# Attention kernel: batch 0's products of probabilities and values, split into three parts

## The chip, the cores and the metric

The kernel runs on one core of a Trainium2 chip. The core has five engines that work side by side, each through its own instructions in a fixed order: TensorE (PE, the matmuls; PEld is its weight loads), VectorE (DVE), ScalarE (ACT), GpSimd (POOL) and SyncE (SP, which here only issues transfers). The metric is the device time of one execution in microseconds. Before the change the median of three runs is 521.31 us (519.27, 521.31 and 526.38). The profiled execution took 525.91 us, of which 524.1 us lie between its first and its last instruction.

## The reference

Four batches, eight heads each, 576 positions, 64 numbers per head, all in float32:

```python
scores = q @ k.T / sqrt(64)
scores = where(causal, -1e9, scores + min(-(cum_i - cum_j), 0))   # cum: running sum of max(s, 0)
attn   = softmax(scores)
x      = attn @ v                       # the heads side by side: 4 x 576 x 512
gate   = sigmoid(conv5(x))              # over the five last positions, per channel
x      = (gate * (x @ w_val)) @ w_out
h      = relu(x @ w_in);  u, v = the two halves of h
out    = (u * (w_spatial @ layernorm(v) + b)) @ w_out2
```

The weights arrive as 64-bit floats. The kernel turns them into float32 on the chip and multiplies `moe_w_out` by `moe2_w_in` once (the "fold"), one half of it in plain float32 (`wo_f`, `wi_f`, line 429), the other half as sums of two reduced-precision numbers.

## The kernel before, in words

The attention runs in **turns**, `w` = 0 to 32, one head each (lines 693 to 733). Turn `w` issues the scores of head `w` and the transposes of head `w - 1`.

*Scores* (lines 190 to 225). A head's 576 queries are cut into five tiles, of 64, 128, 128, 128 and 128 queries. For each, TensorE fills a PSUM bank (`pss`), VectorE adds the mask and finds the row's extreme (line 219, `p` and `nm`), and ScalarE takes the exponential and the row's sum (line 224). The first eight heads, batch 0, multiply in float32 (line 209); the others in two steps (lines 211, 212). The tiles `p` exist twice, for even heads (buffers p_116 to p_120) and odd ones (p_127 to p_131).

*Transposes* (lines 257 to 272). TensorE turns `p` block by block into `pst`, and ScalarE copies it to `pt` (line 272), in four banks: bank 1 and 2 hold the keys 0 to 127 (`c` = 0), bank 3 those of `c` = 2 and 3, bank 0 those of `c` = 1 and 4. There are two `pt`, so the copies for head `h + 2` wait until head `h`'s has been read. A new `p` of head `h + 2` waits for the transposes that read that of head `h`.

*Products with the values* (`pv`, lines 276 to 300) are made for two heads at a time. For every `c` and each head `j` one matmul, with the 64 columns of `vraw` as weights, adds to `pso` (queries 128 to 575: 448, 448, 320, 192 and 64 columns) or makes `psq` (queries 0 to 127); head 0 writes the PSUM partitions 0 to 63 and head 1 the others. Line 294 holds all of them back until the first of them, of `c` = 1 and head 1, can go. VectorE then scales by the inverse sums `R` into `x` (line 300). `R` is transposed to `psr`, copied by ScalarE, written to DRAM (`r_d`, line 242) and read back on SP (line 248). `pso` exists once and `psq` shares one bank with `psr`.

*Behind it.* The convolution reads `x` (lines 309 to 313). The rest (the fold, the gate's product, the mixing) is issued between the pieces of attention by `more`, whose share per turn is a table: 3 in batch 0, then 11.5, 10, 7.6 and 6. During batch 0 it is the preparation of the weights (lines 357 to 409: loads `wg` and `wr` on SP, steps on ScalarE, VectorE and GpSimd), the float32 half of the fold (`fold`, evacuated as `wch` by ScalarE and `wcl` by VectorE) and the first products with `w_val` (`xvh`, `xvl`, lines 417 to 419).

*The order of the work.* The program is written as above, and a scheduler (line 787) then sets the order of each engine's instructions by its own model of their times and by the program's priorities. Each engine runs its list strictly in order, so an instruction that waits holds all behind it.

Of the kernel before, what the change touches and what calls it, by code (L numbers as in the profile page):

```python
# [7 lines left out]
F32 = mybir.dt.float32  # L8
# [4 lines left out]
ALU = mybir.AluOpType  # L13
PSUM = bass.MemoryType.PSUM

NEG = -1.0e30
NATIVE = 8


F64_LOW = 2.0 ** (896 // 8 - 127 + 16)  # L20
# [4 lines left out]
def tile_stickbreak_attention_moe(  # L25
# [18 lines left out]
    NH, S = s.shape  # L44
    B = out.shape[0]
    H = NH // B
# [11 lines left out]
    BLK, w = {}, 0  # L58
# [5 lines left out]
    V, G, A, T, SY = nc.vector, nc.gpsimd, nc.scalar, nc.tensor, nc.sync  # L64
# [162 lines left out]
    R = {}  # L227
# [48 lines left out]
    def pv(h):  # L276

        b, p = h // H, (h % H) // 2
        x = X[b, p] = early.tile([128, S], F32, tag=f"x{p}", name=f"x{p}", bufs=1)
        r = R.pop(h // 2).rearrange("p i q -> p (i q)")  # L280
        pts = [PT.pop(h + j) for j in range(2)]
        vs = [vraw.pop(h + j) for j in range(2)]

        first = None
        for tag, q0, q1 in (("o", 128, S), ("q", 0, 128)):
            po = ps.tile([128, 512], F32, tag=tag, name=f"ps{tag}", bufs=1)
            cs = [1, 0, 2, 3, 4] if q0 else [0]
            for c in cs:
                a = max(q0, c * 128)
                o = BLK[c, c] + a - c * 128  # L290
                for j in (1, 0):
                    with ExitStack() as es:
                        if first is not None:
                            es.enter_context(tc.issue_after(first))
                        m = T.matmul(po[64 * j:64 * j + 64, a - q0:q1 - q0], vs[j][:, c, :], pts[j][:, o:o + q1 - a],  # L295
                                     start=c == cs[0], stop=c == cs[-1])
                    first = first or m.ins
            for a, e in ((q0, 64), (64, q1)) if q0 == 0 else ((q0, q1),):
                o = a + 64 if a else 0
                V.tensor_tensor(out=x[:, a:e], in0=po[:, a - q0:e - q0], in1=r[:, o:o + e - a], op=ALU.mult)  # L300

    Z = {}

# [312 lines left out]
    def more(n):  # L616
        with tc.high_priority(offset=0):
            more_(n)
# [74 lines left out]
    for w in range(NH + 1):  # L693
        if w == H + 1:
            queue.clear()
            queue.append(start())
        elif w % H == 1 and w > 1 and w < NH:
            queue += [mixing_a(w // H - 1), mixing_b(w // H - 1)]
        if w >= NATIVE:
            load(w + 2)  # L700
        n_g = [3, 11.5, 10.0, 7.6, 6.0][0 if w <= H else 1 if w <= H + 4 else 2 if w <= 2 * H else 3 if w <= 3 * H else 4]
        gs = [n_g / 5] * 5
        if w < NH:
            scores(w, [0, 1])
        if w > 0:
            transposes(w - 1, [1, 2])
        if w % 2 == 0 and w > 0:
            lay_sums(w // 2 - 1)
        more(gs[0])
        if w < NH:  # L710
            scores(w, [2])
        prep(w + 1)
        if w > 0:
            transposes(w - 1, [3])
        more(gs[1])
        if w < NH:
            scores(w, [3])
        if w > 0:
            transposes(w - 1, [0])
        if w % 2 == 0 and w > 0:  # L720
            spread_sums(w // 2 - 1)
        more(gs[2])
        if w < NH:
            scores(w, [4])
            if w < NATIVE:
                load(w + 2)
            if w % 2:
                normalise(w // 2)
        more(gs[3])
        if w % 2 == 0 and w > 0:  # L730
            pv(w - 2)
            conv((w - 2) // H, ((w - 2) % H) // 2)
        more(gs[4])
    load_ahead(wo_d, B - 2, ["wv", "wv"])
# [56 lines left out]
```

## Time and profile before

| what | value |
|---|---|
| median of three runs | 521.31 us (519.27 to 526.38) |
| profiled execution | 525.91 us, span 524.1 us |
| PE busy | 495.5 us, 95% |
| PEld busy | 412.9 us, 79% |
| ACT busy | 334.3 us, 64% |
| DVE busy | 312.9 us, 60% |
| POOL busy | 125.1 us, 24% |
| mean granted TensorE clock | 0.977 |

The first row says how much a difference must be to be seen: the three runs lie 7 us apart. Busy shares are means over a program of two halves, with batch 0 (about the first 109 us) unlike the rest, so they are read by stretches. The granted clock is a share of 2.4 GHz; 0.50 is 1.2 GHz.

### The profile page before, as it was taken

How to read it: one execution, taken by the hardware profiler on the slowest of the kernel's cores; microseconds unless marked ns; L12 is line 12 of the kernel's file. 1: busy time of each engine (PE TensorE's matmuls, PEld its weight loads, DVE VectorE, ACT ScalarE, POOL GpSimd, SP SyncE). 2: the span in 40 equal slices, each digit the busy share in tenths (PEclk: the TensorE clock that was granted, in tenths of full speed). 3: DMA queues.
4: the chain of work that ended last, by engine and by line, in shares of the span. 5: the costliest groups of instructions: out<-in, count | busy, mean ns of one | idle time of the engine just before them, and what ended most of it. 6: DMA issues, size and time to landing. Idle time of an engine off the chain costs nothing.

```text
span 524.1 us, 9075 instructions
## 1 busy us (share of the span) xinstructions
PE 495.5 (95%) x3186; PEld 412.9 (79%) x3186; DVE 312.9 (60%) x830; ACT 334.3 (64%) x813; POOL 125.1 (24%) x167
## 2 busy tenths in 40 slices
PE   7789787969999999999999999999999999999997
PEld 5445445558877978989979897899579889998997
DVE  6777877676888878564477644835289544025120
ACT  3997785596685976985648754876279834224322
POOL 5211111014172111300335021002115013046140
PEclk9989997989999999999999999999999999999999
DMA  7837774345546374067631322286220060700002
GB/s 210 272 103 252 232 233 153 107 139 155 151 159 215 89 236 153 3 201 237 202 103 58 107 83 84 60 279 216 77 67 14 26 255 24 240 0 3 1 1 91
DMA packets 28302, 69.26 MB, mean 132 GB/s; under 512 B 4000, under 2 KB 12352, under 8 KB 28256
## 3 DMA queue, kind: packets, MB, share of 16 engines
q1 hardware_dynamic: 23328, 63.88, 39.0%
q10 hardware_dynamic: 4928, 4.80, 2.7%
q8 instruction: 25, 0.41, 0.3%
q14 instruction: 21, 0.17, 0.1%
HBM read 55.96 MB, written 9.16 MB: 124 GB/s over the span
## 4 chain that ended last, share of the span: by engine, by line
PE 64%; DVE 13%; ACT 10%; DMA 8%; issue 3%; POOL 1%; SPq 1%; DVEq 0%; ACTq 0%; POOLq 0%
PE psm L417 11%; PE psm L419 11%; PE psm L418 11%; PE pso L295 7%; PE pst L271 6%; PE psm L593 3%; PE psm L595 3%; PE psm L594 3%; DVE p L219 3%; DVE z L312 2%; ACT p L224 2%; PE pss L211 2%; PE pss L212 2%; DMA R<-r_d 2%; DMA wr<-in_w_out 2%
## 5 line engine op out<-in xcount | busy, mean ns | idle before, releaser
L224 ACT ACTIVATE p<-p,nm 64x64 f32<-64x64 f32 (+4 forms) x160 | 88.4, 553 | 10.0 <-DVE nm L219 9.7
L271 PE MATMUL pst<-ident,p 128*128 128x128 f32 x480 | 81.4, 281 | 9.4 <-ACT p L224 6.0
L272 ACT ACTIVATE pt<-pst 128x512 f32<-128x512 f32 (+1 forms) x128 | 61.0, 497 | 42.7 <-PE psq L295 25.7
L219 DVE CUSTOM_DVE_ANT_0 p<-pss,mask 64x64 f32<-64x64 f32 (+4 forms) x160 | 64.0, 419 | 25.4 <-PE pss L212 15.7
L271 PEld LDWEIGHTS pst<-ident,p 128*128 128x128 f32 x480 | 59.0, 143 | 23.2 <-ACT p L224 10.2
L312 DVE SCALAR_TENSOR_TENSOR z<-x,cw,z 128x575 f32<-128x575 f32 (+3 forms) x64 | 54.3, 854 | 4.7 <-ACT z L309 4.2
L79 POOL TENSOR_TENSOR y<-gt,y 128x288 fp32r<-128x288 f32 x32 | 27.8, 872 | 115.7 <-ACT y L72 115.7
L79 POOL TENSOR_TENSOR g<-gt,g 128x288 fp32r<-128x288 f32 x32 | 27.1, 849 | 104.1 <-ACT g L72 104.0
L295 PE MATMUL pso<-pt,vraw 128*64 128x448 f32 (+3 forms) x320 | 51.8, 431 | 0.0
L211 PE MATMUL pss<-qk 128*64 128x64 f32 (+1 forms) x144 | 46.8, 343 | 1.6 <-DVE nm L219 1.4
L295 PEld LDWEIGHTS pso<-pt,vraw 128*64 128x64 f32 x320 | 23.1, 140 | 25.1 <-issue 17.4
L212 PE MATMUL pss<-kd,cn 66*64 66x64 f32 (+1 forms) x144 | 42.2, 298 | 0.0
L209 PE MATMUL pss<-raw 128*128 128x288 f32 (+4 forms) x96 | 31.2, 425 | 8.0 <-DVE nm L219 7.2
L417 PE MATMUL psm<-g,wch 128*128 128x288 f32 x128 | 38.2, 306 | 0.2 <-ACT u L581 0.2
L593 PE MATMUL psm<-wsh,vh 128*128 128x288 f32 x128 | 38.1, 304 | 0.2 <-ACT u L581 0.2
L595 PE MATMUL psm<-wsl,vh 128*128 128x288 f32 x128 | 37.6, 300 | 0.0
L418 PE MATMUL psm<-g,wcl 128*128 128x288 f32 x128 | 37.4, 298 | 0.0
L594 PE MATMUL psm<-wsh,vl 128*128 128x288 f32 x128 | 37.3, 298 | 0.0
L419 PE MATMUL psm<-g,wch 128*128 128x288 f32 x128 | 37.1, 298 | 0.0
L300 DVE TENSOR_TENSOR x<-pso,R 128x448 f32<-128x448 f32 x16 | 9.9, 622 | 44.5 <-DMA R<-r_d 19.9
L498 DVE TENSOR_TENSOR gt<-psm,z 128x288 f32<-128x288 f32 x32 | 14.2, 452 | 32.7 <-PE psm L419 29.7
L417 PE MATMUL psm<-xvh,wv 128*128 128x288 f32 x96 | 30.6, 322 | 2.7 <-DVE wcl L79 2.7
(168 smaller groups left out, 1324.9 us busy)
## 6 DMA issues: line engine op xcount, KB each, us to landing
raw<-in_qk SPq DMA_DIRECT2D x24, 576.0 KB
wv<-wv_d SPq DMA_DIRECT2D x12, 512.0 KB
wv<-wo_d SPq DMA_DIRECT2D x12, 512.0 KB
vraw<-in_vp SPq DMA_DIRECT2D x32, 160.0 KB
R<-r_d SPq DMA_DIRECT2D x32, 160.0 KB
out<-ot ACTq DMA_DIRECT2D x32, 144.0 KB
cn<-qk SPq DMA_DIRECT2D x24, 144.0 KB
wr<-in_w_in SPq DMA_DIRECT2D x5, 512.0 KB
```

The lines of the kernel that those rows point to most:

```text
L79: eng.tensor_tensor(out=out_, in0=in_, in1=f(hi), op=ALU.subtract)
L211: T.matmul(pst[0:m, o:o + b - a], qa[:, q0:q0 + m], kb[:, a:b], start=True, stop=False)
L219: LAST["V"] = V.tensor_tensor_reduce(out=p[i][0:m, a:b], in0=src, in1=mask[0:m, o:o + b - a], scale=-0.125, scalar=3.0e38 if a == 0 else n ...
L224: A.activation(p[i][0:m, 0:e], p[i][0:m, 0:e], AF.Exp, bias=nm[0:m, i:i + 1], scale=-1.0, accum_out=sm[h // 2 % 2][0:m, h % 2, i:i + 1])
L271: T.transpose(pt[:, o - o0:o - o0 + 128], p[i][:, c * 128:(c + 1) * 128], ident[:, r:r + 128])
L272: A.activation(PT[h][:, o0:end], pt[:, 0:end - o0], AF.Copy)
L295: m = T.matmul(po[64 * j:64 * j + 64, a - q0:q1 - q0], vs[j][:, c, :], pts[j][:, o:o + q1 - a], start=c == cs[0], stop=c == cs[-1])
L312: V.scalar_tensor_tensor(out=z[:, d:], in0=x[:, :S - d], scalar=cw[:, p, k:k + 1], in1=z[:, d:], op0=ALU.mult, op1=ALU.add)
L417: T.matmul(pt, ah, bh, start=j == 0, stop=False)
L418: T.matmul(pt, al, bh, start=False, stop=False)
L419: T.matmul(pt, ah, bl, start=False, stop=j == n - 1)
L593: T.matmul(o, vh[c][:, cs], wsh[:, c, hs[hf]], start=c == 0, stop=False)
```

## The change

Batch 0's four pairs of heads no longer call `pv`. In their turns (`w` = 2, 4, 6, 8) the matmuls of the pair are issued in three parts: those of `c` = 0 (with `psq`) behind the transposes of bank 1 and 2, those of `c` = 2 and 3 behind bank 3, those of `c` = 1 and 4 behind bank 0. The scaling stays where `pv` stood. Within a part head 0 now comes before head 1, the sum begins with `c` = 0 instead of 1, and nothing holds a matmul back until another has gone. The two banks are taken when the first part is issued. From batch 1 on `pv` is as before.

```diff
+PARTS = 8
...
+    PO = {}
+
+    def pv_part(h, cs):
+
+        if h < 0:
+            return
+        if h not in PO:
+            PO[h] = [ps.tile([128, 512], F32, tag=t, name=f"ps{t}", bufs=1) for t in "oq"]
+        po, pq = PO[h]
+        for c in cs:
+            for t, q0, q1 in ((po, 128, S), (pq, 0, 128))[0:2 if c == 0 else 1]:
+                a = max(q0, c * 128)
+                o = BLK[c, c] + a - c * 128
+                for j in range(2):
+                    T.matmul(t[64 * j:64 * j + 64, a - q0:q1 - q0], vraw[h + j][:, c, :], PT[h + j][:, o:o + q1 - a],
+                             start=c == 0, stop=c == 4 or q0 == 0)
+
+    def pv_scale(h):
...
+        for t, q0, a, e in ((po, 128, 128, S), (pq, 0, 0, 64), (pq, 0, 64, 128)):
+            o = a + 64 if a else 0
+            V.tensor_tensor(out=x[:, a:e], in0=t[:, a - q0:e - q0], in1=r[:, o:o + e - a], op=ALU.mult)
...
             transposes(w - 1, [1, 2])
+        parts = w - 2 if w <= PARTS and w % 2 == 0 else -1
         if w % 2 == 0 and w > 0:
             lay_sums(w // 2 - 1)
+        pv_part(parts, [0])
         more(gs[0])
...
             transposes(w - 1, [3])
+        pv_part(parts, [2, 3])
         more(gs[1])
...
             transposes(w - 1, [0])
+        pv_part(parts, [1, 4])
...
         if w % 2 == 0 and w > 0:
-            pv(w - 2)
+            pv(w - 2) if parts < 0 else pv_scale(parts)
             conv((w - 2) // H, ((w - 2) % H) // 2)
```

The instructions of each engine are the same before and after, in number and shape; their order differs on every engine from the first pair on, on TensorE up to about the middle of its list. Lines up to 299 move by 1, later ones by 33; the new matmuls are on line 317, the new scaling on line 333.

**TensorE, the first pair.** Before, its ten matmuls into `pso` stand in one block, the two heads in turn (`pt_299` and `vraw_167` are head 1, `pt_235` and `vraw_163` head 0), between the transposes of head 2:

```order
L271 MATMUL pst_415<-ident_91,p04_120 128x128
L295 MATMUL pso_370<-pt_299,vraw_167 64x448
L295 MATMUL pso_370<-pt_235,vraw_163 64x448
L295 MATMUL pso_370<-pt_299,vraw_167 64x448
L295 MATMUL pso_370<-pt_235,vraw_163 64x448
L295 MATMUL pso_370<-pt_299,vraw_167 64x320
L295 MATMUL pso_370<-pt_235,vraw_163 64x320
L295 MATMUL pso_370<-pt_299,vraw_167 64x192
L295 MATMUL pso_370<-pt_235,vraw_163 64x192
L295 MATMUL pso_370<-pt_299,vraw_167 64x64
L295 MATMUL pso_370<-pt_235,vraw_163 64x64
L271 MATMUL pst_436<-ident_91,p04_120 128x128
```

Now head 0's matmul of `c` = 0 goes alone, a turn earlier, between the transposes of head 1:

```order
L272 MATMUL pst_303<-ident_91,p11_128 128x128
L272 MATMUL pst_303<-ident_91,p12_129 128x128
L317 MATMUL pso_314<-pt_235,vraw_163 64x448
L272 MATMUL pst_333<-ident_91,p12_129 128x128
L210 MATMUL pss_344<-raw0_66 128x448
```

and six of the other nine stand in two groups among head 2's transposes, one head a step ahead of the other; the last three (448 of head 1, 64 of both) follow as a third group five transposes later:

```order
L317 MATMUL pso_314<-pt_299,vraw_167 64x448
L317 MATMUL pso_314<-pt_235,vraw_163 64x320
L272 MATMUL pst_405<-ident_91,p01_117 128x128
L272 MATMUL pst_405<-ident_91,p02_118 128x128
L272 MATMUL pst_405<-ident_91,p03_119 128x128
L272 MATMUL pst_405<-ident_91,p04_120 128x128
L210 MATMUL pss_497<-raw0_66 128x320
L317 MATMUL pso_314<-pt_299,vraw_167 64x320
L317 MATMUL pso_314<-pt_235,vraw_163 64x192
L317 MATMUL pso_314<-pt_299,vraw_167 64x192
L317 MATMUL pso_314<-pt_235,vraw_163 64x448
```

What moved: one matmul to the turn before, and the rest from one block into three groups in the same neighbourhood. The other three pairs have the same groups.

**VectorE, around the scaling of the third pair** (`x_698` before, `x_712` now). Before:

```order
L376 SCALAR_TENSOR_TENSOR wg<-wg 128x512
L300 TENSOR_TENSOR x_698<-pso,R 128x448
L300 TENSOR_TENSOR x_698<-psq,R 128x64 x2
L79 TENSOR_TENSOR qk<-raw_66,qk 64x576
L219 ISA p_131,nm<-pss,mask 128x288
L219 ISA nm 128x1
L376 SCALAR_TENSOR_TENSOR wr<-wa,wr 128x512
L79 TENSOR_TENSOR kd_108<-raw_66,qk 64x576
```

Now:

```order
L409 SCALAR_TENSOR_TENSOR wg<-wg 128x512
L80 TENSOR_TENSOR qk<-raw_66,qk 64x576
L409 SCALAR_TENSOR_TENSOR wr<-wa,wr 128x512
L220 ISA p_130,nm<-pss,mask 128x448
L220 ISA nm 128x1
L80 TENSOR_TENSOR kd_108<-raw_66,qk 64x576
L333 TENSOR_TENSOR x_712<-pso,R 128x448
L333 TENSOR_TENSOR x_712<-psq,R 128x64 x2
L220 ISA p_131,nm<-pss,mask 128x288
L220 ISA nm 128x1
```

What moved: the scaling stands three instructions later, behind `qk`, `wr` and `kd_108`. The first `wcl` after it (the evacuation of the fold's first column) was the twelfth large instruction behind the scaling and is now the sixth, with `qk` and `kd_109` of the next head behind it instead of ahead.

**ScalarE, in the same place.** Before, the step `wr<-wr`, which reads a weight transfer, stands behind both `wch`:

```order
L309 ACTIVATE z<-x_698,cw 128x576
L72 ACTIVATE xvh_928<-x_698 128x576
L72 ACTIVATE qk<-raw_67 128x576 x2
L224 ACTIVATE p_131,sm_113<-p_131,nm 128x576
L252 ACTIVATE wch<-psm 128x512 x2
L379 ACTIVATE wr<-wr 128x512
```

Now it stands between them, ahead of an exponential and of the next head's `qk`:

```order
L342 ACTIVATE z<-x_712,cw 128x576
L73 ACTIVATE xvh_928<-x_712 128x576
L253 ACTIVATE wch<-psm 128x512
L412 ACTIVATE wr<-wr 128x512
L225 ACTIVATE p_131,sm_113<-p_131,nm 128x576
L73 ACTIVATE qk<-raw_67 128x576 x2
L253 ACTIVATE wch<-psm 128x512
```

What moved: a step that waits for a transfer went ahead of four that don't need it. The issue of that transfer on SP moved too, from behind the loads `raw_67` and `cn_107` to ahead of them.

## Rows read from the trace of the kernel before

**Rows 1.** Stretches: length, busy of PE, PEld, DVE, ACT, POOL (count), clock, DMA, GB/s.

```profile
26.00:117.00 91.00, 75.92 (x381) 47.43 (x382) 68.10 (x193) 70.07 (x175) 12.81 (x11) 0.90 0.57 175
117.00:260.00 143.00, 140.28 (x977) 123.57 (x977) 100.21 (x268) 106.27 (x265) 37.53 (x42) 0.99 0.51 161
```

**Rows 2.** PE's waits from 20 to 117 us: total, times, longest.

```profile
PE pss L209 <- DVE nm L219: 7.2, 12, 1.8
PE pst L271 <- ACT p L224: 3.1, 1, 3.1
```

**Rows 3.** Timeline of PE, first pair: start, length, line, matmul, records merged [idle before].

```profile
37.57 4.50 PE L295 MATMUL pso<-pt,vraw 128*64 128x448 f32 x20
```

**Rows 4.** The same view, second pair.

```profile
50.72 2.70 PE L295 MATMUL pso<-pt,vraw 128*64 128x448 f32 x20
```

**Rows 5.** The same view, fifth pair, where single matmuls stand among others.

```profile
131.59 0.29 PE L419 MATMUL psm<-xvl,wv 128*128 128x288 f32 x1
131.82 0.54 PE L295 MATMUL pso<-pt,vraw 128*64 128x192 f32 x2
132.29 0.40 PE L418 MATMUL psm<-xvh,wv 128*128 128x288 f32 x1
132.62 0.33 PE L295 MATMUL pso<-pt,vraw 128*64 128x64 f32 x2
132.88 0.40 PE L419 MATMUL psm<-xvl,wv 128*128 128x288 f32 x1
133.20 0.27 PE L295 MATMUL pso<-pt,vraw 128*64 128x64 f32 x1
133.21 0.32 PE L295 MATMUL psq<-pt,vraw 128*64 128x128 f32 x1
```

**Rows 6.** Stretches, columns as in Rows 1: three at the low clock, two at the high.

```profile
34.00:41.00 7.00, 6.59 (x23) 3.21 (x23) 1.91 (x6) 5.66 (x18) 0.09 (x1) 0.53 0.50 156
46.00:56.00 10.00, 9.43 (x58) 5.46 (x56) 9.66 (x27) 8.85 (x23) 2.69 (x3) 1.00 1.01 300
86.00:92.40 6.40, 5.87 (x18) 4.50 (x19) 2.70 (x10) 3.83 (x11) 0.00 (x0) 0.50 0.33 103
92.40:109.00 16.60, 16.60 (x98) 11.18 (x96) 12.19 (x34) 11.20 (x27) 0.00 (x0) 1.00 0.35 98
113.50:119.20 5.70, 4.28 (x19) 4.28 (x20) 1.79 (x8) 5.69 (x17) 0.47 (x1) 0.50 0.49 184
```

**Rows 7.** Timeline of ACT [idle before <- what ended it].

```profile
42.83 1.20 ACT L272 ACTIVATE pt<-pst 128x64 f32<-128x64 f32 x3 [3.17 <-PE psq L295]
86.60 0.70 ACT L379 ACTIVATE wr<-wr 128x512 int32<-128x512 uint32 x1 [3.52 <-DMA wr<-in_w_in]
```

**Rows 8.** Timeline of DVE, scalings and what stands near them.

```profile
42.47 0.36 DVE L219 CUSTOM_DVE_ANT_0 p<-pss,mask 128x192 f32<-128x192 f32 x1 [6.00 <-PE pst L271]
...
61.48 0.62 DVE L300 TENSOR_TENSOR x<-pso,R 128x448 f32<-128x448 f32 x1 [1.85 <-DMA R<-r_d]
...
76.66 0.62 DVE L300 TENSOR_TENSOR x<-pso,R 128x448 f32<-128x448 f32 x1 [2.58 <-DMA R<-r_d]
...
78.36 0.46 DVE L219 CUSTOM_DVE_ANT_0 p<-pss,mask 128x288 f32<-128x288 f32 x1
...
83.60 0.82 DVE L312 SCALAR_TENSOR_TENSOR z<-x,cw,z 128x574 f32<-128x574 f32 x1
...
85.81 0.67 DVE L79 TENSOR_TENSOR wcl<-psm,wch 128x512 fp32r<-128x512 f32 x1
```

**Rows 9.** Timeline of PE, around the waits near 62 and 86 us.

```profile
62.82 0.75 PE L209 MATMUL pss<-raw 128*128 128x288 f32 x2 [1.59 <-DVE nm L219]
...
86.53 0.61 PE L417 MATMUL psm<-xvh,wv 128*128 128x288 f32 x1 [2.71 <-DVE wcl L79]
...
90.14 4.74 PE L429 MATMUL psm<-wi_f,wo_f 128*128 128x512 f32 x8
```

**Rows 10.** Timeline of SP, the weight transfer that ACT reads at 86.60.

```profile
81.53 0.38 SPq L371 DMA_DIRECT2D wr<-in_w_in  x1
```

More of the change, by code (lines that the diff above doesn't have):

```diff
@@ L300, in pv @@
                 V.tensor_tensor(out=x[:, a:e], in0=po[:, a - q0:e - q0], in1=r[:, o:o + e - a], op=ALU.mult)
+    PO = {}
[13 more added lines that the diff above has]
+    def pv_scale(h):
+        if h < 0:
+            return
+        b, p = h // H, (h % H) // 2
+        po, pq = PO.pop(h)
+        for j in range(2):
+            PT.pop(h + j)
+            vraw.pop(h + j)
+        x = X[b, p] = early.tile([128, S], F32, tag=f"x{p}", name=f"x{p}", bufs=1)
+        r = R.pop(h // 2).rearrange("p i q -> p (i q)")
+        for t, q0, a, e in ((po, 128, 128, S), (pq, 0, 0, 64), (pq, 0, 64, 128)):
+            o = a + 64 if a else 0
+            V.tensor_tensor(out=x[:, a:e], in0=t[:, a - q0:e - q0], in1=r[:, o:o + e - a], op=ALU.mult)
     Z = {}
```

## The prediction, made before the change was run

> **What bounds the kernel now.** I read the table by stretches first [rows 1]: it splits the program into a part that TensorE fills and a part that it doesn't. From 117 to 260 us TensorE is busy for 140.28 of 143 us at clock 0.99, so what happens there hardly moves the end unless TensorE gets more to do. From 26 to 117 us, where batch 0 and the change lie, it is busy for 75.92 of 91 us, and the granted clock is 0.90. So 15.1 us of idle time and about 9 us of lost clock (a tenth of 91) are all that the change could win there, some 24 us, or 4.6% of the run.
>
> Then the waits of TensorE [rows 2]: its pauses from 20 to 117 us are many short ones for VectorE's scan of the scores (7.2 us in 12), and one of 3.1 us for an exponential that stands behind the gate's sigmoid. Third, the timelines around the first block [rows 3, 7, 8]: while TensorE works off the ten products of pair 0 in 4.50 us, ScalarE stands for 3.17 us and VectorE for 6.00 us, both until transposes and `psq` behind the block are through. That is the cost the change can reach. Fourth, the granted clock [rows 6]: three stretches near 0.50 (1.2 GHz), at 34 to 41, 86 to 92.4 and 113.5 to 119.2 us. Each follows a time in which TensorE paused; the second follows the 2.71 us until `wcl` [rows 9]. Last, VectorE's scalings [rows 8]: those of pairs 1 and 2 wait 1.85 and 2.58 us for `R` to come back from DRAM, not for the products.
>
> **The change, part by part.** No instruction is added or removed; all of it is order.
>
> *Products that lose their partner.* In the block head 1 and head 0 alternate, and pair 1's takes 2.70 us at the full clock [rows 4]. It streams 448 + 448 + 320 + 192 + 64 = 1472 columns per head. One product of 192 columns alone keeps TensorE from 131.82 to 132.29, 0.47 us [rows 5]; 2944 columns at that rate would be over 7 us, so in the block the two heads run beside each other, at 2.70 / 1472 = 1.83 ns a column. In the new order head 0's first product is alone (448), head 1's 448 stands with head 0's 320 (448), then 320, 192, 192 and 448 follow with the heads shifted by one (768), then 448 with 64 and 64 (512). I take it that products of different heads still overlap when they are not of one `c`: a `pso` and a `psq` product of different length start 0.01 us apart [rows 5]. The sum is 2176 columns instead of 1472: 704 x 1.83 ns = **1.3 us** more per pair.
>
> *More changes of shape.* Before, a pair had two groups (`pso`, `psq`), now five. What a group costs beyond its columns is read where single products stand among others [rows 5]: 0.47 - 192 x 1.83 ns = 0.12 us, and 0.26 (132.62 to 132.88) - 64 x 1.83 ns = 0.14 us. Three more groups, in and out, are 6 x 0.13 = **0.8 us** per pair. The Trainium skill, in TensorEngine Tiling (Array Packing), under Tiling Modes, Key Properties, says that changing the tiling mode drains TensorE, which speaks against cutting a block up; the rows agree that there is a price. With about 175 ns for a drain, the Trainium skill's figure in TensorE: Matmul & The Clock Gate, under Single matmul latency, the 24 changes would make 4.2 instead of 3.1 us, an estimate that would add 1 us to the sum below at most.
>
> Together 2.1 us per pair, 8.4 us for four. How much of it is on the path:
>
> - The first product (0.82 us and two changes, 1.1 us) goes ahead. Pair 0's falls into the pauses for the scan [rows 2], pair 3's into the 2.71 us before `wcl` [rows 9]. That leaves 1.0 us per pair in the old place.
> - Pair 0: there the clock is 0.53 [rows 6] and the block took 4.50 instead of 2.70 us, so 1.0 becomes 1.6 us. ScalarE and VectorE both wait for what is behind it [rows 7, 8], and that is not released earlier: `psq` and the transposes of `p_117` are still behind all of the products. **+1.6**, bounds 0 and +3.5.
> - Pair 1: VectorE is busy for 9.66 of 10 us from 46 to 56 us [rows 6] and sets the pace. **0**, at most +2.1.
> - Pair 2: its first product waits for pair 1's scaling, which ends at 62.1 us [rows 8]; TensorE is idle from 61.2 to 62.82 anyway [rows 9]. The product and the transposes behind it push the scores by about 0.8 us. The 2.58 us wait for `R` behind it [rows 8] hides this: **0**, at most +1.8.
> - Pair 3: TensorE is busy for all of 92.4 to 109 us [rows 6]. **+1.0**, bounds 0 and +2.1.
>
> *VectorE around pair 2's scaling.* The scaling now has `qk`, `wr` and `kd_108` ahead of it, which fill the wait for `R` (three steps of 0.67 to 0.82 us, like those in rows 8, into 2.58 us); it still goes at 76.66 us. Behind it six instead of twelve steps stand ahead of `wcl`: five of 0.46 to 0.82 us from 77.6 us, so `wcl` starts at about 81 instead of 85.81 us [rows 8], before TensorE comes for its bank at 83.8 us. The 2.71 us pause at that place goes [rows 9]. What is late next: ScalarE now reads the transfer `wr` between the two `wch`. It takes 86.60 - 81.53 = 5.07 us from issue to use [rows 7, 10]; with `wr` and `kd_108` done earlier on VectorE, SP can issue it at about 77 us, and it lands at 82. ScalarE stands for some 3 us, in place of the 3.52 it stood [rows 7], with an exponential, `qk` and the second `wch` queued behind. The second bank then comes free at about 87 us, and the fold's third column, at 90.14 us before [rows 9], can follow at about 87.4. **-2.7**; at worst 0, if the wait for `wr` is the longer one; at best -2.7 and the clock too: 5.87 us of work at 0.50 [rows 6] would take half, another -2.9.
>
> *The sigmoid* moves some exponentials later in ScalarE's list. The pause of 3.1 us [rows 2] and the low clock behind it (4.28 us of work, 2.1 lost [rows 6]) can end better or worse by as much. **0**, bounds -5.2 and +3.
>
> Sum: +1.6 + 1.0 - 2.7 = -0.1 us on 525.9 us, the profiled execution's time (1.8 us outside its span), which lies 4.6 us above the median. On the median that is **521 us: no change that could be told**, since 2% of it, 10.4 us, is about what a measurement of this kernel can tell from none. This case's own range, with one or two of the bounds above at their ends, is 515 to 526.
>
> **The rivals.**
>
> 1. *Slower: the first product holds TensorE.* `pso` exists once, so head 0's early product must wait for the scaling of the pair before, which waits for `R`; TensorE then stands in front of transposes that it used to make in that time. For: two scalings wait for `R` [rows 8]. Against: at both, TensorE or VectorE idles as it is. Price: pair 2 waits from about 60.6 to 62.1 us, 1.5 us. It decides once the wait is as long as the 2.71 us after which the clock was at 0.50 for 6.4 us [rows 6, 9], that is with `R` 1.2 us later; then each hold costs about 2.7 + 2.9 us. One such hold, the products' 2.6 and no gain at `wcl` make +8.2; two make +13.8. Time 529 to 535, say 531.
>
> 2. *Faster: TensorE keeps its clock.* If the shorter pauses leave the clock up, 34 to 41 us gives 3.1 us (6.59 us of work, 0.47 of it lost), 86 to 92.4 us 2.9, 113.5 to 119.2 us 2.1 [rows 6], and the pause before `wcl` 2.7: -10.8, and +2.6 for the products, so 513. Against: the first of them begins before the groups that moved, and only one lone product stands in front of it.
>
> 3. *Nothing happens.* `pso` and `psq` are still finished last, ScalarE's copies for the next head still wait for `psq` [rows 7], and a scheduler has put the groups where the block was. Then the array time is hidden or small, with the reshuffled work behind it as the only difference: 521 to 523.
>
> **How the numbers follow.** The forecast has 0.55, rival 1 0.15, rival 2 0.18, rival 3 0.12. The likeliest time is 521. Rivals 2 and 3 and the low end of the sigmoid's bound reach 512, rival 1 with one hold 530; beyond these lie two holds or all three clocks at once with the sigmoid's pause, less than 2 in 10. Range 512 to 530. Faster by over 2% (below 510.9) needs rival 2 and more: 0.08. Slower by over 2% (above 531.7) is rival 1 with more than one hold: 0.09. Within 2%: 0.83.
>
> **What would show it.** Right: the ten products of a pair take about 3.6 to 4.8 us in all at the full clock; VectorE's wait in front of `p_117` is still near 6 us; no wait in front of pair 2's scaling; TensorE's pause before the first `xvh` product is gone, and ScalarE waits about 3 us for `wr` ahead of the second `wch`. Wrong: a TensorE wait of over 2 us for a scaling in front of a product with 448 columns (rival 1); a clock of 1.00 from 34 to 41 us (rival 2); or a difference that arises after 120 us, where only the scheduler's order of the same work could make it.

## The result, and the profile after

The changed kernel takes **525.67 us** (median of 20 runs, 523.35 to 530.29) against 521.88 us for the kernel before in the same comparison (519.27 to 526.38): a ratio of 1.0072, 95% interval 1.0046 to 1.0098. It is slower by 0.7%, which is within 2% and told apart from no change. The profiled execution of before was one with much time at the low clock, so a second one of the same kernel (`base`, below) stands beside it here: 518.71 us, span 516.9. Runs over 1.5% above the fastest of their kernel (three of before, one of `mid_b`) are left out of all medians and means below.

The head of the page of the changed kernel:

```profile
span 524.0 us, 9074 instructions
## 1 busy us (share of the span) xinstructions
PE 500.2 (95%) x3186; PEld 409.6 (78%) x3186; DVE 316.6 (60%) x830; ACT 334.0 (64%) x813; POOL 127.2 (24%) x167
```

Stretches of the changed kernel, columns as in [rows 1], the last one a spell at the low clock:

```profile
34.00:41.00 7.00, 7.00 (x35) 3.48 (x34) 1.77 (x7) 6.00 (x19) 0.00 (x0) 0.76 0.28 88
86.00:92.40 6.40, 6.40 (x32) 3.29 (x30) 1.75 (x6) 3.79 (x11) 0.00 (x0) 1.00 0.38 135
113.50:119.20 5.70, 5.70 (x48) 5.11 (x44) 4.82 (x15) 5.69 (x13) 1.91 (x2) 1.00 0.28 65
26.00:117.00 91.00, 83.53 (x429) 49.38 (x428) 71.38 (x202) 74.05 (x184) 13.10 (x12) 0.96 0.53 175
117.00:260.00 143.00, 139.22 (x946) 121.97 (x946) 102.00 (x262) 104.26 (x260) 40.91 (x44) 0.99 0.54 167
215.00:225.00 10.00, 8.44 (x50) 7.47 (x49) 5.86 (x21) 9.97 (x25) 0.80 (x1) 0.83 0.47 121
```

The same two long stretches of `base`:

```profile
26.00:117.00 91.00, 78.11 (x436) 52.21 (x437) 74.43 (x208) 76.37 (x193) 16.71 (x16) 0.96 0.59 187
117.00:260.00 143.00, 141.17 (x972) 121.33 (x970) 99.35 (x261) 102.15 (x252) 36.42 (x42) 1.00 0.53 164
```

Until 117 us the changed kernel keeps TensorE busy for 5.4 us more than `base`, at the same mean clock, with nearly as many matmuls done (429 records against 436): more time for the work, fewer pauses. From 117 to 260 us it gets 26 matmul records less done in the same time. That is where it falls behind. Followed matmul by matmul, each counted at its mean cost over the two traces, the changed kernel is 1.0 us behind `base` at 117 us, 0.5 at 190 and 7.8 at 260; from 307 us of `base` on, TensorE's order is the same in both. For what `base` does from 190 to 260 us it takes 7.3 us more: 4.1 of work (1.9 in the products of pairs 7 to 9, seven pieces more, and 1.4 in the matmuls next to pieces), 1.6 of pauses and 1.6 of low clock.

TensorE's waits of the changed kernel from 20 to 117 us (line, engine waited for, us, times, longest), the answer to [rows 2]:

```profile
PE pss L210 <- DVE nm L220: 2.7, 5, 1.1
PE pss L212 <- DVE nm L220: 2.0, 2, 1.4
...
PE pso L317 <- PE pst L272: 0.7, 1, 0.7
```

Its products of pair 0 in the old place (three rows), all of pair 1 (five) and the early one of pair 2, in the timeline of TensorE, the answers to [rows 3, 4]. Two records (x2) are one product:

```profile
33.96 1.40 PE L317 MATMUL pso<-pt,vraw 128*64 128x448 f32 x4
...
37.40 1.46 PE L317 MATMUL pso<-pt,vraw 128*64 128x320 f32 x8
...
39.48 1.08 PE L317 MATMUL pso<-pt,vraw 128*64 128x448 f32 x6
...
45.28 0.97 PE L317 MATMUL pso<-pt,vraw 128*64 128x448 f32 x2
...
48.41 0.97 PE L317 MATMUL pso<-pt,vraw 128*64 128x448 f32 x4
...
50.54 1.30 PE L317 MATMUL pso<-pt,vraw 128*64 128x320 f32 x8
...
53.06 1.08 PE L317 MATMUL pso<-pt,vraw 128*64 128x448 f32 x6
...
54.77 0.44 PE L317 MATMUL psq<-pt,vraw 128*64 128x128 f32 x4
...
59.94 0.94 PE L317 MATMUL pso<-pt,vraw 128*64 128x448 f32 x2 [0.67 <-PE pst L272]
```

Its first product with `xvh` and the fold's third column, the answer to [rows 9]:

```profile
82.66 0.29 PE L450 MATMUL psm<-xvh,wv 128*128 128x288 f32 x1
...
85.18 3.70 PE L462 MATMUL psm<-wi_f,wo_f 128*128 128x512 f32 x8 [0.63 <-DVE wcl L80]
```

The same place in `base`, where the wait for `wcl` stands in front of the first `xvh` product:

```profile
81.19 0.40 PE L417 MATMUL psm<-xvh,wv 128*128 128x288 f32 x1 [1.82 <-DVE wcl L79]
...
83.21 3.60 PE L429 MATMUL psm<-wi_f,wo_f 128*128 128x512 f32 x8
```

ScalarE and VectorE of the changed kernel at the places of [rows 7, 8]:

```profile
41.44 1.20 ACT L273 ACTIVATE pt<-pst 128x64 f32<-128x64 f32 x3 [1.44 <-PE psq L317]
...
80.46 0.68 ACT L412 ACTIVATE wr<-wr 128x512 int32<-128x512 uint32 x1 [2.50 <-DMA wr<-in_w_in]
```

```profile
40.97 0.36 DVE L220 CUSTOM_DVE_ANT_0 p<-pss,mask 128x192 f32<-128x192 f32 x1 [4.16 <-PE pst L272]
...
75.23 0.61 DVE L333 TENSOR_TENSOR x<-pso,R 128x448 f32<-128x448 f32 x1
...
79.51 0.68 DVE L80 TENSOR_TENSOR wcl<-psm,wch 128x512 fp32r<-128x512 f32 x1
```

ScalarE and VectorE behind the first block in `base`, where the clock is 1.00 from 34 to 41 us:

```profile
39.97 1.20 ACT L272 ACTIVATE pt<-pst 128x64 f32<-128x64 f32 x3 [0.97 <-PE psq L295]
```

```profile
39.61 0.36 DVE L219 CUSTOM_DVE_ANT_0 p<-pss,mask 128x192 f32<-128x192 f32 x1 [3.70 <-PE pst L271]
```

Up to here most goes the way of the forecast. What the forecast has no row for comes later. Pair 9 (the tenth) in the changed kernel, TensorE; `psm` rows between the products are left out, the last row is the one behind them:

```profile
259.71 0.97 PE L296 MATMUL pso<-pt,vraw 128*64 128x448 f32 x4
...
261.27 1.83 PE L296 MATMUL pso<-pt,vraw 128*64 128x448 f32 x10
...
264.16 0.54 PE L296 MATMUL pso<-pt,vraw 128*64 128x192 f32 x2
...
265.06 0.33 PE L296 MATMUL pso<-pt,vraw 128*64 128x64 f32 x2
...
265.75 0.33 PE L296 MATMUL pso<-pt,vraw 128*64 128x64 f32 x2
...
266.68 0.43 PE L296 MATMUL psq<-pt,vraw 128*64 128x128 f32 x2
...
267.47 0.43 PE L296 MATMUL psq<-pt,vraw 128*64 128x128 f32 x2
...
267.83 0.50 PE L450 MATMUL psm<-wch,g 128*128 128x512 f32 x1
```

The scheduler has cut these twelve products into seven **pieces** (runs of products with no other matmul between them) among the gated block's matmuls; in the kernel before it were three. In the whole trace the changed kernel has 60 pieces, 19 in batch 0 and 41 behind it; the kernel before has 42, that is 7 and 35. From pair 13 on the order is the same in both. Its first product starts at 370.75 us in the changed kernel (of a span of 524.0, so 153.25 before the end) and at 363.30 us in `base` (of 516.9, 153.6 before the end): all of the loss is made ahead of it.

In between, the changed kernel's TensorE waits for an exponential; the stretch around it is the last one (215 to 225 us, clock 0.83) of the changed kernel's above:

```profile
218.86 0.47 PE L272 MATMUL pst<-ident,p 128*128 128x128 f32 x1 [1.21 <-ACT p L225]
```

Measured in the two traces from each matmul's start to the next one's, with the idle time before the next one counted as a pause and the low clock at half speed taken out, TensorE's work grew by 10.4 us (484.8 to 495.2), its pauses fell by 4.3 (23.4 to 19.1), and the low clock took 1.0 more (4.0 to 5.0): +7.05 us, the difference of the spans. Of the work, batch 0's products have 5.6 us (11.85 to 17.4), the later products 1.3 (41.55 to 42.85), and the other matmuls 3.5, most of it in those that stand next to pieces.

### The profile page after: what moved, and what is told of

Read it like the earlier page. It is cut to its first block, busy times and chain, and to the rows that moved or that the text cites. A ratio compares the mean times of both kernels' runs of the same rounds, so it can differ in the third digit from the quotient of the medians.

```text
span 524.0 us, 9074 instructions
## 1 busy us (share of the span) xinstructions
PE 500.2 (95%) x3186; PEld 409.6 (78%) x3186; DVE 316.6 (60%) x830; ACT 334.0 (64%) x813; POOL 127.2 (24%) x167
## 5 line engine op out<-in xcount | busy, mean ns | idle before, releaser
L345 DVE SCALAR_TENSOR_TENSOR z<-x,cw,z 128x575 f32<-128x575 f32 (+3 forms) x64 | 56.6, 891 | 4.6 <-ACT z L342 4.2
L80 POOL TENSOR_TENSOR g<-gt,g 128x288 fp32r<-128x288 f32 x32 | 28.7, 902 | 118.6 <-ACT g L73 118.2
L296 PE MATMUL pso<-pt,vraw 128*64 128x448 f32 (+3 forms) x240 | 41.3, 436 | 0.0
L531 DVE TENSOR_TENSOR gt<-psm,u 128x288 f32<-128x288 f32 x32 | 14.5, 455 | 32.2 <-PE psm L630 23.3
L450 PE MATMUL psm<-y,wv 128*128 128x288 f32 x96 | 29.8, 311 | 3.9 <-ACT ot L641 3.6
L296 PEld LDWEIGHTS pso<-pt,vraw 128*64 128x64 f32 x240 | 17.5, 140 | 19.7 <-issue 13.7
```

Source lines behind the costliest of these rows:

```text
L80: eng.tensor_tensor(out=out_, in0=in_, in1=f(hi), op=ALU.subtract)
L345: V.scalar_tensor_tensor(out=z[:, d:], in0=x[:, :S - d], scalar=cw[:, p, k:k + 1], in1=z[:, d:], op0=ALU.mult, op1=ALU.add)
L450: T.matmul(pt, ah, bh, start=j == 0, stop=False)
```

## The experiments

Theory A: the end shows the products of batch 0, which take 5.6 us more (5.1 in an expectation below). Theory B: that cost is covered by shorter pauses, and the end shows the order behind batch 0.

Every run comes with its mean granted clock. At half speed below full, (1 - clock) x span is the time lost to the low clock; the mean time less this is called *at full clock* here (for the changed kernel 525.97 - 4.75 = 521.2). In the four comparisons that list its clock the kernel before had 513.6 to 514.3, so tenths are noise, and a kernel's runs scatter by 0.6 to 2.6 us (standard deviation). By the runs the figure takes off too much: from run to run of one kernel, 1 us more of that loss goes with only 0.55 us more of time (95% interval 0.45 to 0.65, from 234 runs in 20 groups); why is not shown. So where two kernels differ in clock, what their orders differ by lies between the difference of the times and that at full clock.

| kernel | pieces, batch 0 + later | median us | ratio (95%) | clock | at full clock |
|---|---|---|---|---|---|
| before | 7 + 35 | 521.6 to 522.6 | 1 | 0.985 | 513.6 to 514.3 |
| the change | 19 + 41 | 525.67 | 1.0072 (1.0046 to 1.0098) | 0.991 | 521.2 |
| serial | 7 + 37 | 525.34 | 1.0064 (1.0033 to 1.0094) | 0.985 | 517.6 |
| pair | 14 + 45 | 532.05 | 1.0195 (1.0151 to 1.0239) | 0.988 | 525.2 |
| parts2 | 9 + 36 | 523.91 | 1.0040 (1.0011 to 1.0069) | 0.983 | 514.7 |
| parts6 | 16 + 55 | 530.35 | 1.0164 (1.0119 to 1.0210) | 0.991 | 526.1 |
| c0first | 7 + 35 | 521.34 | 0.9993 (0.9962 to 1.0023) | 0.985 | 513.7 |
| whole_b | 7 + 12 | 515.88 | 0.9875 (0.9838 to 0.9913) | 0.981 | 505.8 |
| whole_a | 19 + 13 | 508.52 | 0.9742 (0.9704 to 0.9781) | 0.996 | 506.5 |
| mid_b | 7 + 31 | 523.75 | 1.0064 (1.0027 to 1.0101) | 0.981 | 515.1 |
| mid_a | 19 + 33 | 520.99 | 0.9998 (0.9965 to 1.0032) | 0.992 | 517.3 |
| tail_b | 7 + 18 | 511.02 | 0.9806 (0.9757 to 0.9855) | 0.986 | 504.0 |
| tail_a | 19 + 24 | 517.20 | 0.9909 (0.9873 to 0.9944) | 0.989 | 511.7 |
| whole4 | 13 + 12 | 512.58 | 0.9829 (0.9783 to 0.9874) | 0.981 | 503.2 |
| p9_a | 19 + 38 | 524.81 | 1.0063 (1.0033 to 1.0092) | 0.992 | 521.0 |
| early_b | 7 + 12 | 514.82 | 0.9849 (0.9804 to 0.9894) | 0.980 | 504.0 |
| early_a | 19 + 13 | 512.94 | 0.9843 (0.9791 to 0.9894) | 0.989 | 508.2 |

**base**, the kernel before once more, without an edit.

> The kernel before, once more, for a second profile of it. The profile shown has 23.9 us at the low clock, the changed kernel's 10.2 us. If the clock alone made that profile long, this one shows a time near 522 us with less of it, and the TensorE work between (busy time less pauses, at the full clock) is again near 485 us, against 495 us in the changed kernel. If instead the work differs from run to run by several us, the comparison of the two profiles says little.

518.71 us at clock 0.99, against 525.9 in the first profile. TensorE's work is the same from one execution to the other (485.2 and 484.8 us), and so are the pauses (23.9 and 23.4); the low clock took 10.3 us in the one and 4.0 in the other.

**serial**, the kernel before with the heads of a block one after the other in batch 0:

```
-            for c in cs:
+            for c, j in ([(c, j) for j in (1, 0) for c in cs] if h < H else [(c, j) for c in cs for j in (1, 0)]):
...
-                for j in (1, 0):
+                if True:
```

> The kernel before with one thing changed: in batch 0's four blocks head 1's five products come first and then head 0's, so that no two run beside each other. The order of everything else stays the same to 99%. TensorE has 1472 columns more per pair, at 1.83 ns 2.7 us, 10.8 us in four pairs. Theory A (TensorE's time for the products in batch 0 is on the path): slower by 5 to 11 us, 527 to 533. Theory B (it is covered, and the change lost its time in the new order of the work behind batch 0): 522 to 524.

Batch 0's products take 20.2 us instead of 11.85, 8.4 more, with the rest of the order hardly touched (two pieces more behind batch 0); the pauses fall by 6, and at full clock 4.0 of the 8.4 reach the end (517.6 against the 513.6 of this comparison). So batch 0's pauses cover about half of what is put under them. The time, 525.34, lies between the two theories' ranges.

**pair**, the change with head 1 first and the rest of a part held behind it, so that partners stay together:

```
+        first = None
...
-                for j in range(2):
...
+                for j in (1, 0):
+                    with ExitStack() as es:
+                        if first is not None:
+                            es.enter_context(tc.issue_after(first))
...
+                    first = first or m.ins
```

> The changed kernel with the partners kept: within each part head 1 comes first and the others are held until it has gone, as the block did. The parts stand where the change put them. Theory A: the 1.3 us per pair of lost overlap are saved, 5 us of TensorE time, and 2 to 5 us of them show: 521 to 524. Theory B: the order behind batch 0 is still another one, so the time stays near 525.7, 524 to 528.

Batch 0's products fall to 12.87 us, nearly the kernel before's, so most of the 5.6 us were lost partners (it has five pieces fewer there, too); and the kernel is the slowest of all, 532.05 us, outside both theories' ranges. Behind batch 0 it has 45 pieces (pair 9 alone ten), and at full clock it takes 11.6 us more than the kernel before. Followed matmul by matmul as above, it is level with `base` at 117 us (1.3 us behind) and 15 us behind at 280. That the time goes up when the partners come back speaks against theory A, and the place of the loss for B. Against the changed kernel, though, the traces show no more work (494.2 against 495.2 us) but longer pauses, 25.0 against 19.1 us: the order costs by its waits here, not by pieces alone.

**parts2**, the change for the first pair alone (`PARTS = 2`).

> The changed kernel with only the first pair in parts, the other three in blocks as before. Theory A: a quarter to a half of the change's cost (the first pair stands where ScalarE and VectorE wait for it): 523 to 524. Theory B: the order behind it decides, not the number of pairs: anything from 520 to 527, with TensorE's work for the products longer by only 1.4 us.

Two pieces more in batch 0 and one behind it: 1.0 us at full clock against the 513.6 of the same comparison, and some 1 us more of low clock. 523.91 us lies in both ranges, so this run decides nothing.

**parts6**, the change for the first three pairs (`PARTS = 6`).

> The change for the first three pairs only; the scheduler then cuts the products of the later pairs into some 55 pieces against 35 before and 41 with the change. Theory A (cost by pairs in parts: 2 us for one, 3.8 for four): between, 3.3 us above the kernel before, 525 us. Theory B (pieces behind batch 0 decide, some 0.2 to 0.4 us each): 5 to 10 us above, 526 to 531 us, although fewer pairs are in parts than in the changed kernel.

530.35 us: fewer pairs in parts than in the changed kernel, but 55 pieces behind batch 0, and 4.7 us slower. Theory B said 526 to 531.

**c0first**, the null: two steps of the sum exchanged in batch 0's blocks (`[1, 0, 3, 2, 4]` for `[1, 0, 2, 3, 4]`).

> The kernel before with only the order of two products inside batch 0's blocks exchanged (the third and fourth 64-column matmul groups); no other engine's order and no block moves. Either theory: 521 to 522 us, the same as before within 0.3%. It shows how much of a difference of a few tenths of a per cent is nothing at all.

Same, as both expected.

**whole_b** and **whole_a**, the kernel before and the changed one with the later pairs' products raised in the scheduler's priority, so that each pair's twelve stand together:

```
                         if first is not None:
                             es.enter_context(tc.issue_after(first))
+                        if h >= H:
+                            es.enter_context(tc.high_priority(offset=150))
```

> The kernel before, in which the twelve products of each pair of batches 1 to 3 are raised in the scheduler's priority, so that they stand on TensorE in one piece (before, these 12 pairs are cut into 35 pieces among the gated block's matmuls and take 41.5 us of TensorE; a pair in one piece takes 2.85). Batch 0 is left as it is. Theory B (what the change lost after 190 us is the order of the work behind batch 0, with its pieces and their changes of shape): the products fall to 12 x 2.85 = 34.2 us, 7.3 less, and the neighbours' changes of shape some 2 less; half to all of it reaches the end: 513 to 518 us. Theory A (only batch 0's cost counts, what is behind is covered by pauses): 521 to 522, with longer pauses.

> The changed kernel with the same raised priority for the products of batches 1 to 3: batch 0 in three parts as the change has it, everything behind it in whole blocks. Theory B: with the pieces behind batch 0 gone on both sides, what is left between this and whole_b is batch 0's own cost as far as it reached the end before 190 us, 0 to 1.5 us; the gap of 3.8 us closes. Theory A (batch 0's 5.1 us more of products is what the end shows): this stays 3 to 5 us above whole_b.

Both gain, some 7 and 17 us. The gap doesn't only close, as B said: the changed kernel comes out 7.4 us *ahead*, which neither theory has. At full clock the two are 0.7 us apart, and the clock is 0.996 against 0.981; by the 0.55 from above, that difference is worth some 4 of the 7.4 us.

What a piece costs is read at pair 13, which stands in twelve pieces in both kernels. In `base`, the first two products, the first and the last of the `psm` matmuls between, and the next work:

```profile
363.30 0.97 PE L295 MATMUL pso<-pt,vraw 128*64 128x448 f32 x2
364.20 0.40 PE L418 MATMUL psm<-xvh,wv 128*128 128x288 f32 x1
364.53 0.97 PE L295 MATMUL pso<-pt,vraw 128*64 128x448 f32 x2
...
373.35 0.40 PE L419 MATMUL psm<-xvl,wv 128*128 128x288 f32 x1
373.68 0.43 PE L295 MATMUL psq<-pt,vraw 128*64 128x128 f32 x2
374.04 0.24 PE L211 MATMUL pss<-qk 128*64 128x64 f32 x1
```

The same pair in `whole_a`, with two of the `psm` matmuls ahead of it:

```profile
359.76 0.29 PE L452 MATMUL psm<-xvh,wv 128*128 128x288 f32 x1
359.90 0.29 PE L453 MATMUL psm<-xvh,wv 128*128 128x288 f32 x1
...
360.41 2.70 PE L298 MATMUL pso<-pt,vraw 128*64 128x448 f32 x20
362.94 0.39 PE L298 MATMUL psq<-pt,vraw 128*64 128x128 f32 x4
363.27 0.40 PE L453 MATMUL psm<-xvh,wv 128*128 128x288 f32 x1
```

In pieces, pair 13 and the eleven `psm` matmuls among it last from 363.30 to 374.04, 10.74 us. Together the products take 2.86 us (360.41 to 363.27), and eleven `psm` one after another 11 x 0.14 = 1.5. So eleven pieces more cost 6.4 us, 0.58 each. `serial` takes that apart, for there the products have no partner either, but stand together; its first pair's ten, which take 2.70 us in `base`:

```profile
38.68 4.79 PE L295 MATMUL pso<-pt,vraw 128*64 128x448 f32 x20
```

Where a pair's twelve products stand in one piece, from the first start to the next work, they take 2.85 us with partners, 4.95 without (`serial`, pair 3), and 7.13 in twelve pieces (10.74 less eleven times 0.33). So of the 6.4 us about a third is the lost partners (4.95 - 2.85 = 2.1), a third is paid by the products for standing singly among others (7.13 - 4.95 = 2.2), and a third by their neighbours: a `psm` between products takes 0.33 us to the next start instead of 0.14. The last two thirds, some 0.2 us each way, are the price of a change of shape. The Trainium skill's rule that a changed tiling mode drains TensorE (TensorEngine Tiling (Array Packing), under Tiling Modes, Key Properties) agrees with these two.

**mid_a**, **tail_a**, **tail_b**: the raise for some pairs only; `H <= h < 20` in mid_a are pairs 4 to 9, `h >= 20` in the two others pairs 10 to 15:

```
-                        if h >= H:
+                        if H <= h < 20:
```

> The changed kernel with the raised priority only for the products of pairs 4 to 9 (the first pair is 0), where the change cuts them into 18 pieces; pairs 10 to 15, with 7 and 12 pieces in two of them, as in both kernels. If what the change loses arises in pairs 4 to 9 (theory B, the place that the two traces show, 190 to 275 us): back to the kernel before, 519 to 522.5 us, 3 to 6 below the changed kernel. If the changed kernel loses by batch 0's products (theory A): 525 to 526.

> The changed kernel with the raised priority only for the products of pairs 10 to 15, whose pieces stand alike in both kernels. By the trace of whole_a these 19 pieces too many are worth 10 us between 320 and 390 us: 515 to 517 us by theory B, which counts pieces wherever they stand; theory A has no reason for a gain: 523 to 526.

> The kernel before with the same raise for pairs 10 to 15 alone; the pieces of pairs 4 and 9 (4 and 3) stay. Theory B: 10 us off, 511 to 513 us, so that tail_a stays about 4 us behind it, as the change behind before: the loss sits in pairs 4 to 9 and is not touched by this. If the two meet, the loss lies in the tail after all.

They came out near what theory B said: mid_a and tail_b in its ranges, tail_a 0.2 us above its own and 6.2 us behind tail_b instead of some 4. In mid_a pair 9 stands together, behind `psm` matmuls that follow each other in 0.23 us:

```profile
254.74 0.40 PE L452 MATMUL psm<-wch,g 128*128 128x512 f32 x1
254.97 0.39 PE L453 MATMUL psm<-wch,g 128*128 128x512 f32 x1
...
255.53 2.70 PE L298 MATMUL pso<-pt,vraw 128*64 128x448 f32 x20
258.06 0.39 PE L298 MATMUL psq<-pt,vraw 128*64 128x128 f32 x4
258.38 0.50 PE L452 MATMUL psm<-wch,g 128*128 128x512 f32 x1
```

The twelve products take 2.85 us to the next start. In the changed kernel pair 9 and the eleven `psm` among it last 8.12 us (259.71 to 267.83); less 2.85 and 11 x 0.23 = 2.5, that leaves 2.8 us for six pieces more, 0.46 each. The changed kernel is back level with the one before (0.9998) although batch 0 is as the change has it. At full clock, the raise in pairs 10 to 15, which both kernels cut alike, is worth 10.2 us to the one (17 pieces fewer) and 9.5 to the other (17 fewer as well), and the 3.9 us in pairs 4 to 9 come on top: 9.5 + 3.9 = 13.4 of the 14.7 that whole_a has.

**whole4**, whole_a with `PARTS = 4`.

> The change for the first two pairs alone, products of the other batches whole as in whole_a. A candidate for the fastest: if parts give batch 0 shorter pauses pair by pair, it lies between whole_b (515.9) and whole_a (508.5), 511 to 514 us; if what whole_a gains on whole_b is the luck of an order, anything from 506 to 518.

512.58 us, between whole_b and whole_a, as forecast, but the 506 to 518 of the other reading holds it too. At full clock it has the lowest figure (503.2, not told apart from the 504.0 of tail_b and early_b), but it loses 9.6 us to the clock, and whole_a 2.3. The fastest kernel of all that were run is whole_a: it beats the kernel before by 2.6% in one comparison, the changed one by 3.3% across two.

**p9_a**, **mid_b**, **early_a**, **early_b** ask what of the order costs: the pieces, or pauses that come with it. p9_a raises pair 9 alone (`h == 18`), mid_b pairs 4 to 9 in the kernel before, and the last two are whole_a and whole_b with `offset=None`, the highest priority.

> The changed kernel with the raised priority for one pair alone, the tenth (pair 9, seven pieces in the changed kernel, three before). By pieces: its products fall from 4.4 to 2.85 us and six changes of shape of the neighbours at 0.18 us go, 2.6 us in all, which is most of what the changed kernel lost in that stretch: 522.5 to 523.5 us. If pieces cost nothing by themselves and only some other property of the order does: 525 to 526.

> The kernel before with the raise for pairs 4 to 9 alone, which has seven pieces there and gains little by it. whole_b stands 4.9 us behind tail_b although it has fewer pieces; its trace has 4.3 us more of pauses. If the raise in these pairs brings pauses whatever stands behind: 525 to 528. If that loss belongs to the order of whole_b alone: 519 to 522, since five pieces fewer are worth 1 to 2 us.

> whole_a with the highest priority in place of a middling one: the same pieces (one for each later pair but the first), another order of the work around them. If pieces set the time: 508.5 as whole_a, within 2 us. If whole_a is a lucky order: 512 to 518.

> whole_b with the highest priority: the same pieces, another order. By pieces alone 511 to 513 (12 fewer in pairs 10 to 15 are worth 10 us, by tail_b); with the pauses that whole_b showed, 515 to 517. Together with early_a it shows how far the order, at equal pieces, moves the end.

p9_a is a miss. Pair 9 now stands together, but the scheduler then cuts pair 10 into four pieces instead of one; three pieces fewer give 0.2 us at full clock (0.9 in the mean times), which can't be told from none. mid_b, between its two ranges, loses 1.2 us at full clock with four pieces fewer: its trace has 1.8 us less of work and 1.9 us more of pauses than `base`, and more of the low clock. early_a lies 1.7 us above whole_a at full clock and 4.4 in all, early_b 1.8 and 1.1 below whole_b, with the same pieces. early_a so falls into the range that its expectation has for "a lucky order", early_b lies between its two, and of whole_a's 7.4 us ahead of whole_b 1.9 are left between early_a and early_b. So the order at equal pieces is worth some 2 us, and its clock as much again.

Taken together, over the 17 kernels of the table the time at full clock rises with the pieces by 0.47 us each (a straight line through them), and none lies more than 3.5 us off it. With a slope of its own for each place, a piece behind batch 0 goes with 0.51 us and one in batch 0 with 0.26; on the plain mean times, with nothing taken off for the clock, with 0.48 and -0.1. So the price behind batch 0 doesn't hang on how the clock is counted, and that of batch 0 does. The four kernels that lie highest have a reason in their trace: serial has products without partners, mid_b, whole_b and pair have longer pauses.

## Why the prediction was wrong, point by point

The time, 525.67, lies in the range, and the sign is not the forecast's "no change": 0.7% is told apart. With 20 runs of each kernel the interval is 0.5% wide, not the 2% that the forecast took for what can be told from none.

- *Products that lose their partner, and changes of shape* (1.3 + 0.8 us per pair, 8.4 in all): right, and near in size. In pair 1 the ten products take 0.97 + 0.97 + 1.30 + 1.08 = 4.32 us in four rows after 2.70 in one [rows 4], within the 3.6 to 4.8 us forecast. Rows overlap at their ends, though: from start to next start batch 0's products, `psq` among them, take 5.6 us more. In `pair`, with the partners back and five pieces fewer, 4.6 of it are gone, 1.1 per pair of heads. With the matmuls next to them, which the forecast's "in and out" includes and which take some 1.8 us more in batch 0, it is 7.4 us instead of 8.4.
- *What of it is on the path*: right in sum. The pauses that were to cover the products did: those for the float32 scan went from 7.2 us in twelve [rows 2], 6.3 in eleven in `base`, to 2.7 in five, and at 117 us the changed kernel is 1.0 us behind `base`.
- *Pair 0*: +1.6 us, at a clock of 0.53, can't be checked, since the clock was 0.76 from 34 to 41 us. The three groups in the old place take 1.40 + 1.46 + 1.08 = 3.94 us, ScalarE waits 1.44 us and VectorE 4.16. That is less than the 4.50, 3.17 and 6.00 of [rows 3, 7, 8], but those are of the low clock: in `base`, at 1.00, the block takes 2.70 us and the waits are 0.97 and 3.70. So the waits are 0.5 us longer than there; the direction was right, but the 6 us for VectorE, which were to show the forecast right, came in part from the low clock.
- *Pair 2's scaling*: right. It has no wait in front of it now (1.68 us in `base`), and goes at 75.23 us.
- *The pause before `xvh`*: right. It is gone, `wcl` runs at 79.51 (forecast: about 81), ScalarE waits 2.50 us for `wr` (forecast: some 3), and the fold's third column starts at 85.18 us (forecast: about 87.4) instead of 90.14. Much of that is the clock again: in `base` the pause is 1.82 us and the column starts at 83.21, 2.0 earlier than in the changed kernel, which had lost 1.7 us to the low clock by then.
- *Rival 1*: its mechanism is there, once, as 0.67 us of waiting in front of pair 2's early product, far from the 2.7 from which it was to decide. (The row names the transposes, which end at 59.27 us; pair 1's scaling ends at 59.83 and the product starts at 59.94.)
- *Rival 2*: in part. From 86 to 92.4 and from 113.5 to 119.2 us the clock is 1.00, not 0.50 [rows 6]. One execution proves little: in `base` it is 1.00 there too. But over all runs the kernel with parts has the higher clock in each of the five couples of the table (the change, whole, mid, tail, early), by 0.003 to 0.015, or 1.5 to 7.7 us of clock loss.
- **The step that failed** is the first one of the reading: that what happens from 117 to 260 us "hardly moves the end unless TensorE gets more to do" [rows 1], after which the sum has no term for that stretch. TensorE did get more to do there. The change moved nothing behind batch 0 by hand, but the scheduler placed the same products in 41 pieces instead of 35, with pair 9 in seven, and for what `base` does from 190 to 260 us it took 7.3 us more, 4.1 of them work. With the pieces of pairs 4 to 9 gone, mid_a is 3.9 us faster at full clock and 4.6 in mean time. The order also brought a pause of 1.21 us within 10 us at a mean clock of 0.83 (215 to 225 us), 1.7 us lost; that this spell of low clock comes from the order is not shown. The rows with single matmuls among others [rows 5] were read for a price, and the price was then used for batch 0 alone. The last sentence of the prediction names this as what would make it wrong, "a difference that arises after 120 us", and rival 3 gives it no more than 2 us; its size is 3.9 us at full clock by mid_a. The missing term is that of the seven pieces more in pairs 7 to 9, which measure 3.3 us (1.9 in the products, 1.4 beside them), 0.47 each.

How much batch 0 itself costs at the end is not settled to a figure, nor to a sign. The five couples (a kernel with batch 0 in parts less its twin without) differ at full clock by 7.2 (the change), 7.7 (tail), 2.2 (mid), 0.7 (whole) and 4.2 us (early), in mean time by 3.8, 6.3, -3.5, -7.0 and -0.3. In the last three the pieces of pairs 4 to 9 are gone from both, and there the clock outweighs what is left of the cost.

## What to carry to other kernels

Where a scheduler orders the work, a change at one place is also a change of all that is scheduled after it: compare the two orders to the end, and price what differs there by rows, here 0.46 to 0.58 us for each more piece into which products are cut. A stretch in which an engine is busy for 98% of the time is the one in which such a cut costs its full price; in a stretch with pauses about half of it or more is hidden (`serial`). And before tuning the busy place further, hold together what belongs together there: two lines that raise a priority were worth 7 us, and with the change 17 in one order and 13 in another with the same pieces, where the change alone lost 4.

## What was not expected of the hardware

- Two executions of one program differed by 6.3 us of low clock (10.3 and 4.0 us) at equal work and pauses, so a single profiled execution should be compared by work, pauses and clock apart.
- A pause of 1.21 us, ended by an exponential, stands in the changed kernel in the midst of 10 us at a mean clock of 0.83; the pause ahead of a low clock that the forecast had looked at was 2.71 us long [rows 9].
- In all five couples the kernel with batch 0 in parts has the higher mean granted clock, in `whole` 0.996 against 0.981. That shorter pauses in batch 0 raise it is not shown: no run changed the pauses alone, and whole4 (0.981), parts2 (0.983) and pair (0.988), which have parts too, show little or nothing of it.
- Time does not follow the low clock one to one: from run to run of one kernel, 1 us more of (1 - clock) x span goes with 0.55 us more of time, so that a correction at full price favours the kernels with the lower clock.
